# Two kilobytes of each w_gate partition moved from SyncE's DMA queue to GpSimd's, in loads of 100, 20 and 8 rows

## The chip, the cores and the metric

The kernel runs on one core of a Trainium2 chip (trn2). Such a core has TensorE (PE), which multiplies matrices, VectorE (DVE), ScalarE (ACT), GpSimd (POOL) and SyncE (SP), and 16 DMA engines that carry data between the chip's memory (HBM) and the on-chip memory of 128 partitions (SBUF). A DMA is issued by SP, ACT or POOL, and each of them has a queue of its own onto the DMA engines. The metric is device time in microseconds (us) of one execution; lower is better.

## The reference

One token of a decoder block, everything in fp32: LayerNorm, attention over a cache of 65536 positions with 8 key/value heads and 4 query heads to each, a residual, a second LayerNorm, and a gated feed-forward layer with no nonlinearity in it. `norm` stands for the LayerNorm of the reference.

```python
D, Hq, Hkv, Sk, Dh, F = 512, 32, 8, 65536, 128, 1792
q = norm(x) @ wq                       # 32 query heads of 128
scores = einsum("bhqd,bhkd->bhqk", q, repeat(k_cache, 4)) * Dh ** -0.5
o = einsum("bhqk,bhkd->bhqd", softmax(scores), repeat(v_cache, 4))
h = x + o.reshape(1, 1, Hq * Dh) @ wo
n = norm(h)
h2 = h + ((n @ w_gate) * (n @ w_up)) @ w_down
```

Keys and values are 256 MiB each; all else together is under 30 MiB.

## The kernel before

**Main part.** TensorE runs one loop of eight turns, one for each key/value head (`head()`, L330 to L388). In each turn four tiles of keys (line L343) and four of values (L371) are read, each tile 128 partitions by 64 KB, through two buffers `kv[0]` and `kv[1]`. SP issues the loads of these tiles (L131, and L127 for the last tile of values, which comes in four pieces cut by `V_CUTS`), each as soon as TensorE has read the tile before last in the same buffer. Between the key tiles and the value tiles lies a softmax shared by ACT, DVE and PE.

**The tail.** After the last head the two buffers are used again for the feed-forward weights. `wg_t` and `wu_t` (w_gate and w_up) lie in `kv[0]`, `wd_t` (w_down) in `kv[1]`. In `wg_t` a partition holds 28 KB, which is four blocks `k` of 1792 floats. SP issues w_gate as one DMA (L137) once PE has finished the third value tile of the last head (`pe_at(LAST, M_V + 2)`), and right behind it w_up in three pieces (L140); w_down follows in five pieces (L144) once PE has finished the fourth value tile. The pieces are cut by `U_CUTS` and `D_CUTS`, and each has a semaphore of its own.

TensorE's order in the tail is written out by hand: the second LayerNorm (L393, L395), `project()` with w_gate (L406, which waits for `s_wg` ahead of its first matmul), the variance (L412), a residual term (L414), `project()` with w_up (L406 again, with a wait for each piece), a transposition of the product (L418 to L425), four filling matmuls (L312), and the product with w_down (L437), which waits for each piece of w_down in turn. DVE copies the result (L297) and SP stores it (L299). SP then clears the semaphores, which ends the program.

**GpSimd.** Its work is all at the start: it fills the identity matrix and the padded tiles (L147 to L155), and it has no instruction after that. It issues no DMA. The only DMA that isn't SP's is the load of `x_row` by ACT (L109).

Of the kernel before, what the change touches and what calls it, by code (L numbers as in the profile page):

```python
# [8 lines left out]
P = 128  # L9
D = 512  # L10
# [5 lines left out]
KT = D // P  # L16
F = 1792
# [4 lines left out]
LAST = HKV - 1  # L22
PE_ONLY = bass.OrderedEngineSet([mybir.EngineType.PE])
V_CUTS = (0, 16, 24, 28, 32)
U_CUTS = (0, 2, 3, 4)
D_CUTS = (0, 6, 10, 12, 13, 14)


M_Q, M_K, M_MX, M_MB, M_T, M_L, M_V, M_PO, M_AT, M_HEAD = 1, 2, 6, 7, 8, 12, 13, 17, 18, 18
# [11 lines left out]
        return self.n  # L41


def body(nc, xr, kT, v, wq0, wqo, wo7, wg, wu, wd, out):
    pe_e, dve_e, act_e, pool_e, sp = nc.tensor, nc.vector, nc.scalar, nc.gpsimd, nc.sync

    def tile(name, *shape, align=32):
        return nc.alloc_sbuf_tensor(name, list(shape), F32, align_bytes=align).ap()
# [12 lines left out]
    f_pad = tile("f_pad", P, NC, 32)  # L61
    sel_pad = tile("sel_pad", P, 32)
    zeros = tile("zeros", P, 512)

    kv = [tile(f"kv{i}", P, CK, align=1024) for i in range(2)]
    wqo_sb = tile("wqo_sb", P, 2, KT, 512, align=1024)
# [22 lines left out]
    def sem(name):  # L89
        sems.append(nc.alloc_semaphore(name))  # L90
        return sems[-1]

    pe, dve, act, pool = (Counter(sem(n)) for n in ("pe", "dve", "act", "pool"))
    tok, atok = sem("tok"), sem("atok")
    s_kv = [sem("s_kv0"), sem("s_kv1")]
    s_wq, s_w = sem("s_wq"), sem("s_w")
    s_vp = [sem(f"s_vp{i}") for i in range(len(V_CUTS) - 1)]
    s_wg = sem("s_wg")
    s_wu = [sem(f"s_wu{i}") for i in range(len(U_CUTS) - 1)]
    s_wd = [sem(f"s_wd{i}") for i in range(len(D_CUTS) - 1)]  # L100
    s_xr, s_out = sem("s_xr"), sem("s_out")
    wg_t, wu_t = kv[0][:, 0:KT * F], kv[0][:, KT * F:2 * KT * F]
    wd_t = kv[1]

    def pe_at(h, m):
        return M_HEAD * h + m


    act_e.dma_start(x_row, xr).then_inc(s_xr, 16)  # L109

# [2 lines left out]
    for h in range(HKV):  # L113
        for i in range(2 * NT):
# [9 lines left out]
            if h == LAST and i == 2 * NT - 1:  # L124
                for p, (lo, hi) in enumerate(zip(V_CUTS, V_CUTS[1:])):
                    cs = slice(lo * 512, hi * 512)
# [7 lines left out]
                    sp.sem_inc(p, 16)  # L134
            done.append(pe_at(h, M_K + i if i < NT else M_V + i - NT))
    sp.wait_ge(pe.sem, pe_at(LAST, M_V + 2))
    sp.dma_start(wg_t, wg).then_inc(s_wg, 16)  # L137
    for p, (lo, hi) in enumerate(zip(U_CUTS, U_CUTS[1:])):
        cs = slice(lo * F, hi * F)
        sp.dma_start(wu_t[:, cs], wu[:, cs]).then_inc(s_wu[p], 16)  # L140
    sp.wait_ge(pe.sem, pe_at(LAST, M_V + 3))
    for p, (lo, hi) in enumerate(zip(D_CUTS, D_CUTS[1:])):
# [7 lines left out]
        out=ident, in_=ident, compare_op=ALU.not_equal, fill=1.0, base=0,  # L150
# [2 lines left out]
        c_zero = pool.tick(pool_e.memset(t, 0.0))  # L153
    for t in (o_pad, hn_pad, f_pad, sel_pad, acc):
        c_pads = pool.tick(pool_e.memset(t, 0.0))  # L155

    def dve_self():
        dve_e.wait_ge(dve.sem, dve.n)
# [16 lines left out]
        out=xd, in0=x_col, scalar1=ln_m[:, 0:1], scalar2=None, op0=ALU.subtract))  # L175
# [10 lines left out]
        out=xn, in0=xd, scalar1=ln_r[:, 0:1], scalar2=None, op0=ALU.mult))  # L186
# [3 lines left out]
        out=sel_h, in_=ident.rearrange("p (g h) -> p h g", h=REP), axis=AX.X, op=ALU.add))  # L190
    dve.tick(dve_e.tensor_reduce(
        out=sel_b, in_=ident.rearrange("p (j c) -> p c j", j=4)[:, 0:16, :], axis=AX.X, op=ALU.add))
# [5 lines left out]
        out=neg_mean, in0=mean_m, scalar1=sel_1[:, 0:1], scalar2=-1.0, op0=ALU.mult, op1=ALU.mult))  # L198
# [7 lines left out]
    for h in range(HKV):  # L206
# [7 lines left out]
        for s in range(NT):  # L214
# [11 lines left out]
            out=mrow, in_=sm[1][0:1, 0:P].rearrange("p (g h) -> p h g", h=REP), axis=AX.X, op=ALU.max))  # L226
# [4 lines left out]
            out=nbias, in0=sm[0][:, 0:1], scalar1=-SCALE, scalar2=None, op0=ALU.mult))  # L231
# [6 lines left out]
        for s in range(NT):  # L238
# [7 lines left out]
            out=l4, in0=sel_h, scalar1=l1[:, 0:1], scalar2=None, op0=ALU.mult).then_inc(tok, 1)  # L246
# [7 lines left out]
            out=o_pad[:, :, 0], in0=sm[0][:, 0:REP], in1=linv, op=ALU.mult).then_inc(tok, 1)  # L254
# [12 lines left out]
        out=arow, in0=attn, scalar=1.0, in1=acc, op0=ALU.mult, op1=ALU.add, accum_out=rsum[:, 0:1]))  # L267
    dve_self()
    c_nmean = dve.tick(dve_e.tensor_scalar(
        out=nmean, in0=neg_mean, scalar1=rsum[:, 0:1], scalar2=None, op0=ALU.mult))  # L270
# [16 lines left out]
    for half in range(2):  # L287
        cs = slice(half * 256, min(FJ, half * 256 + 256))
        c_f.append(dve.tick(dve_e.scalar_tensor_tensor(
            out=f_sb[:, cs], in0=psc[0][:, cs], scalar=ln_r3[:, 0:1], in1=g_sb[:, cs],  # L290
# [6 lines left out]
    c_y = dve.tick(dve_e.tensor_copy(y, pva[:, 0:P]))  # L297
    sp.wait_ge(dve.sem, c_y)
    sp.dma_start(out, y[0:P:32, :]).then_inc(s_out, 16)  # L299
    sp.wait_ge(s_out, 16)  # L300

    nums = [s.num for s in sems]
# [27 lines left out]
    def head():  # L330
# [33 lines left out]
        for n in range(NT):  # L364
            vt = kv[n % 2]
            pieces = list(zip(V_CUTS, V_CUTS[1:])) if n == NT - 1 else [(0, 32)]
            for p, (lo, hi) in enumerate(pieces):
# [30 lines left out]
    def project(acc, w, sems):  # L398
        for k in range(KT):
            if len(sems) == 1 and k == 0:  # L400
                pe_e.wait_ge(sems[0], 16)
            elif len(sems) > 1 and k in U_CUTS:
                pe_e.wait_ge(sems[U_CUTS.index(k)], 16)
            for j in range(4):
                o = k * F + j * FJ
                i = mm(acc[32 * j:32 * j + 32, :FJ], hn_pad[:, k, :], w[:, o:o + FJ],  # L406
                       start=(k == 0), stop=(k == KT - 1))
        i.then_inc(pe.sem, 1)

    project(psc[1], wg_t, [s_wg])  # L410
    pe_e.wait_ge(dve.sem, c_s3)
    mm(sm[0][:, 0:1], mean_m, ln_s3, start=True, stop=True).then_inc(pe.sem, 1)  # L412
    for j in range(4):
        mm(pva[32 * j:32 * j + 32, 0:P], sel_pad, arow[:, j * P:(j + 1) * P], start=True, stop=False)  # L414
    project(psc[0], wu_t, s_wu)
    pe_e.wait_ge(dve.sem, c_f[0])
    for b in range(2):
# [63 lines left out]
```

## Time and profile before

| what | value |
|---|---|
| time, median of 3 runs | 1309.85 us (1309.78 to 1309.93) |
| profiled execution, its own time | 1309.92 us |
| its span in the trace | 1308.5 us |
| data read from HBM | 564.66 MB, 432 GB/s over the span |
| TensorE, matmuls | busy 712.9 us, 54% of the span |
| DVE, ACT, POOL | busy 73.5, 47.2 and 2.5 us |
| mean granted clock of TensorE | 0.738 |

The page divides the span into 40 slices and gives for each the busy share of the engines and of the 16 DMA engines. "SPq" is SP in its role as a DMA queue's issuer, "ACTq" that of ACT. The chain of waits follows the last instruction back through what released each step. A row of the windows view gives, for one stretch, the busy time and number of instructions of each engine, the granted clock of TensorE, the mean busy share of the 16 DMA engines and the rate in GB/s. "q1", "q8" and so on are queues on the DMA engines; the kind "instruction" is the fetch of program code.

### The profile page before, as it was taken

How to read it: one execution, taken by the hardware profiler on the slowest of the kernel's cores; microseconds unless marked ns; L12 is line 12 of the kernel's file. 1: busy time of each engine (PE TensorE's matmuls, PEld its weight loads, DVE VectorE, ACT ScalarE, POOL GpSimd, SP SyncE). 2: the span in 40 equal slices, each digit the busy share in tenths (PEclk: the TensorE clock that was granted, in tenths of full speed). 3: DMA queues.
4: the chain of work that ended last, by engine and by line, in shares of the span. 5: the costliest groups of instructions: out<-in, count | busy, mean ns of one | idle time of the engine just before them, and what ended most of it. 6: DMA issues, size and time to landing. Idle time of an engine off the chain costs nothing. (4 is left out here: it accounts for less than half of the span.)

```text
span 1308.5 us, 10559 instructions
## 1 busy us (share of the span) xinstructions
PE 712.9 (54%) x4938; PEld 249.0 (19%) x4938; DVE 73.5 (6%) x181; ACT 47.2 (4%) x102; POOL 2.5 (0%) x13
## 2 busy tenths in 40 slices
PE   5366384553755446563564636636365465655556
PEld 3012031210312112120131202212021121311113
DVE  0000000100001000010000100001000010000101
ACT  0000000100001000010000100001000010000100
POOL 0000000000000000000000000000000000000000
PEclk9777666776767867767767867678677677687778
DMA  9999999999999999999999999999999999999998
GB/s 417 427 435 445 421 445 425 441 425 441 425 441 425 441 429 441 441 429 437 429 439 427 441 425 441 427 441 437 435 435 431 439 417 450 425 441 425 441 420 374
DMA packets 12260, 564.80 MB, mean 432 GB/s; under 512 B 1365, under 2 KB 1369, under 8 KB 2010
## 3 DMA queue, kind: packets, MB, share of 16 engines
q1 hardware_dynamic: 12248, 564.67, 99.7%
q8 instruction: 6, 0.10, 0.0%
q14 instruction: 4, 0.03, 0.0%
q10 hardware_dynamic: 2, 0.00, 0.0%
HBM read 564.66 MB, written 0.00 MB: 432 GB/s over the span
## 5 line engine op out<-in xcount | busy, mean ns | idle before, releaser
L343 PE MATMUL psc<-kv,q_pad 128*32 128x512 f32 x2048 | 294.6, 740 | 256.2 <-PEq L315 256.2
L371 PE MATMUL pva<-kv,pt 128*16 128x512 f32 x2048 | 280.1, 707 | 276.9 <-PEq L315 276.8
L343 PEld LDWEIGHTS psc<-kv,q_pad 128*32 128x32 f32 x2048 | 81.3, 133 | 463.0 <-issue 463.0
L371 PEld LDWEIGHTS pva<-kv,pt 128*16 128x16 f32 x2048 | 67.1, 110 | 492.7 <-issue 492.7
L210 ACT COPY sc<-psc 128x512 f32<-128x512 f32 x32 | 18.7, 585 | 1144.3 <-PE psc L343 1144.3
L216 DVE TENSOR_REDUCE mx<-sc 128x1 f32<-128x512 f32 x32 | 21.9, 686 | 538.3 <-ACT sc L210 538.3
L333 PEld LDWEIGHTS sm<-xn,wqo_sb 128*128 128x128 f32 x256 | 49.1, 299 | 10.4 <-issue 10.4
L333 PE MATMUL sm<-xn,wqo_sb 128*128 128x1 f32 x256 | 49.8, 329 | 2.2 <-issue 2.2
L250 DVE COPY orow<-pva 128x512 f32<-128x512 f32 x8 | 5.5, 692 | 566.8 <-PE pva L371 566.8
L358 PE MATMUL ptp<-ident,sc 128*128 128x128 f32 x128 | 29.3, 396 | 10.2 <-PEq L315 9.7
L358 PEld LDWEIGHTS ptp<-ident,sc 128*128 128x128 f32 x128 | 21.4, 202 | 15.5 <-issue 14.7
L235 ACT ACTIVATE sc<-sc,nbias 128x512 f32<-128x512 f32 x32 | 22.7, 711 | 20.2 <-DVE nbias L230 20.2
L240 DVE COPY pt<-ptp 128x512 f32<-128x512 f32 x32 | 22.1, 691 | 21.6 <-PE ptp L358 21.6
L363 PE MATMUL pva<-zeros 128*32 128x512 f32 x64 | 12.9, 890 | 0.0
L384 PE MATMUL attn<-wqo_sb,o_pad 128*32 128x512 f32 x64 | 10.8, 749 | 3.4 <-PEq L315 3.4
L378 PE MATMUL sm<-sel_b,orow 128*128 128x4 f32 x64 | 8.2, 252 | 7.2 <-PEq L315 7.2
L378 PEld LDWEIGHTS sm<-sel_b,orow 128*128 128x128 f32 x64 | 7.7, 191 | 14.4 <-issue 14.4
L349 PE MATMUL sm<-ident,m 128*1 128x128 f32 x8 | 2.2, 269 | 13.6 <-PEq L315 13.6
L406 PE MATMUL psc<-kv,hn_pad 128*32 128x448 f32 x64 | 8.2, 651 | 1.9 <-DMA kv<-in_wu 1.0
L361 PE MATMUL sm<-l,ones 128*128 128x4 f32 x16 | 3.9, 312 | 9.6 <-PEq L315 9.6
L351 PE MATMUL sm<-ones,mexp 1*128 1x1 f32 x16 | 3.4, 279 | 5.7 <-PEq L315 5.7
L235 ACT ACTIVATION_READ_ACCUMULATOR sc<-sc,nbias 128x1 f32 x32 | 6.0, 187 | 0.0
(88 smaller groups left out, 68.6 us busy)
## 6 DMA issues: line engine op xcount, KB each, us to landing
wqo_sb<-in_wqo SPq DMA_DIRECT2D x7, 2048.0 KB, 15.2
kv<-in_v SPq DMA_DIRECT2D x1, 4096.0 KB, 21.7
kv<-in_wg SPq DMA_DIRECT2D x1, 3584.0 KB, 18.8
kv<-in_v SPq DMA_DIRECT2D x1, 2048.0 KB, 26.2
kv<-in_v SPq DMA_DIRECT2D x2, 1024.0 KB, 29.1
kv<-in_wu SPq DMA_DIRECT2D x1, 1792.0 KB, 23.0
kv<-in_wu SPq DMA_DIRECT2D x2, 896.0 KB, 25.5
kv<-in_wd SPq DMA_DIRECT2D x1, 1536.0 KB, 19.7
```

Source lines behind the costliest of these rows:

```text
L210: copies.append(act.tick(act_e.copy(sc[s], psc[s % 2])))
L216: i = dve_e.tensor_reduce(out=mx[:, s:s + 1], in_=sc[s], axis=AX.X, op=ALU.max)
L235: act_e.activation(sc[s], sc[s], AF.Exp, bias=nbias[:, 0:1], scale=SCALE, accum_out=sums[:, s:s + 1]).then_inc(atok, 1)
L240: dve_e.tensor_copy(pt[s].rearrange("p g b h -> p b g h"), ptp[s % 2].rearrange("p (b g h) -> p b g h", b=4, h=REP)).then_inc(tok, 1)
L333: i = mm(sm[0][:, r:r + 1], wq_sb[:, k, r * P:(r + 1) * P], xn[:, k:k + 1], start=(k == 0), stop=(k == KT - 1))
L343: i = mm(psc[s % 2][32 * j:32 * j + 32, :], q_pad[:, 28 - 4 * rs:60 - 4 * rs], kv[s % 2][:, (4 * rs + j) * 512:(4 * rs + j + 1) * 512], st ...
L358: i = pe_e.transpose(ptp[s % 2][:, b * P:(b + 1) * P], sc[s][:, b * P:(b + 1) * P], ident)
L363: mm(pva[32 * j:32 * j + 32, :], zeros[:, 0:32], zeros, start=True, stop=False)
L371: i = mm(pva[32 * j:32 * j + 16, :], pt[n][:, 8 * j + rs, :, :].rearrange("p b h -> p (b h)"), vt[:, w * 512:(w + 1) * 512], start=False, ...
L378: i = mm(sm[0][:, 0:REP], orow[:, b * P:(b + 1) * P], sel_b[:, 4 * b:4 * b + 4], start=(b == 0), stop=(b == 3))
L384: i = mm(attn[32 * r:32 * r + 32, :], o_pad[:, r, :], wo_sb[:, r, :], start=True, stop=True)
L406: i = mm(acc[32 * j:32 * j + 32, :FJ], hn_pad[:, k, :], w[:, o:o + FJ], start=(k == 0), stop=(k == KT - 1))
```

## The change

Of each partition's 28 KB of w_gate, 26 KB are still loaded by SP, and 2 KB by GpSimd. A partition's row is seen as two halves of 14 KB (`halves`). SP's load takes the first 13 KB of both halves, still as one DMA, and GpSimd's take the last 1 KB of both. GpSimd's part is cut by partitions into three loads, of rows 0 to 99, 100 to 119 and 120 to 127. Ahead of each goes a tiny load of 13, 6 and 6 rows of 32 bytes (two runs of 16 bytes each) from a view of x into a tile `spare` that nobody reads. GpSimd waits for the same point of TensorE's count as SP does for w_gate. The wait of `project()` for w_gate becomes two: one for `s_wg`, one for the three loads of `s_wx`. At the end of the program SP also waits for the tiny loads.

```diff
+SHARED = KT * F // 2 - 256
+EXTRA = ((0, 100), (100, 120), (120, P))
...
+    spare = tile("spare", 16, len(EXTRA), 2, 2 * KT)
...
+    def halves(t):
+        return t.rearrange("p (a f) -> p a f", a=2)
...
     sp.wait_ge(pe.sem, pe_at(LAST, M_V + 2))
-    sp.dma_start(wg_t, wg).then_inc(s_wg, 16)
+    sp.dma_start(halves(wg_t)[:, :, :SHARED], halves(wg)[:, :, :SHARED]).then_inc(s_wg, 16)
...
+    pool_e.wait_ge(pe.sem, pe_at(LAST, M_V + 2))
+    for n, (lo, hi) in enumerate(EXTRA):
+        r = 6 if n else 13
+        pool_e.dma_start(spare[0:r, n, :, 0:KT], xq[0:r]).then_inc(s_sp, 16)
+        pool_e.dma_start(halves(wg_t)[lo:hi, :, SHARED:], halves(wg)[lo:hi, :, SHARED:]).then_inc(s_wx, 16)
...
     sp.dma_start(out, y[0:P:32, :]).then_inc(s_out, 16)
+    sp.wait_ge(s_sp, 16 * len(EXTRA))
     sp.wait_ge(s_out, 16)
...
             if len(sems) == 1 and k == 0:
                 pe_e.wait_ge(sems[0], 16)
+                pe_e.wait_ge(s_wx, 16 * len(EXTRA))
...
+        "xq": lay(A_x, D // 8, 2, 4),
```

More of the change, by code (lines that the diff above doesn't have):

```diff
@@ L41, in tick, with body @@
         return self.n
-def body(nc, xr, kT, v, wq0, wqo, wo7, wg, wu, wd, out):
+def body(nc, xr, xq, kT, v, wq0, wqo, wo7, wg, wu, wd, out):
     pe_e, dve_e, act_e, pool_e, sp = nc.tensor, nc.vector, nc.scalar, nc.gpsimd, nc.sync
@@ L100, in body @@
     s_wd = [sem(f"s_wd{i}") for i in range(len(D_CUTS) - 1)]
-    s_xr, s_out = sem("s_xr"), sem("s_out")
+    s_xr, s_out, s_wx, s_sp = (sem(n) for n in ("s_xr", "s_out", "s_wx", "s_sp"))
     wg_t, wu_t = kv[0][:, 0:KT * F], kv[0][:, KT * F:2 * KT * F]
```

## The prediction

> **What bounds the kernel now.** I read the page first: its slices, its DMA queues and its chain of waits.
>
> ```profile
> span 1308.5 us, 10559 instructions
> ...
> DMA  9999999999999999999999999999999999999998
> ...
> q1 hardware_dynamic: 12248, 564.67, 99.7%
> q8 instruction: 6, 0.10, 0.0%
> q14 instruction: 4, 0.03, 0.0%
> ...
> DMA kv<-in_wd 2%; SPq L144 0%; PE pva L371 0%; PE pva L437 0%; DVE y L297 0%
> ```
>
> The DMA engines are busy from the first slice to the last, nearly all of it with SP's queue (q1). So the time is that of the transfers, and what an edit can change is how many bytes there are (they stay the same) and how the 16 engines come to their end. The chain of waits in order of time shows that end.
>
> ```profile
> 1283.06 22.84 DMA kv<-in_wd
> 1305.90 0.04 issue
> 1305.94 0.47 PE pva L437 x8
> 1306.41 0.02 issue
> 1306.44 0.29 DVE y L297
> ```
>
> The last piece of w_down lands at 1305.90; four matmuls, a copy and the store follow, 2.6 us to the end of the span, and the change touches none of them. The windows view, in steps of a fifth of a microsecond, shows how the engines get there; the column before the last is their mean busy share.
>
> ```profile
> 200.00:1255.00 1055.00, 567.84 (x3883) 191.16 (x3883) 57.10 (x128) 37.60 (x84) 0.00 (x0) 0.73 1.00 434
> 1303.00:1304.00 1.00, 0.53 (x20) 0.53 (x24) 0.00 (x0) 0.00 (x0) 0.00 (x0) 1.00 1.00 393
> 1304.00:1304.20 0.20, 0.20 (x18) 0.20 (x12) 0.00 (x0) 0.00 (x0) 0.00 (x0) 1.00 0.97 338
> 1304.20:1304.40 0.20, 0.20 (x16) 0.09 (x4) 0.00 (x0) 0.00 (x0) 0.00 (x0) 1.00 0.48 184
> 1304.40:1304.60 0.20, 0.16 (x8) 0.00 (x0) 0.00 (x0) 0.00 (x0) 0.00 (x0) 1.00 0.46 174
> 1304.60:1304.80 0.20, 0.10 (x4) 0.11 (x8) 0.00 (x0) 0.00 (x0) 0.00 (x0) 1.00 0.37 143
> 1304.80:1305.00 0.20, 0.20 (x12) 0.20 (x15) 0.00 (x0) 0.00 (x0) 0.00 (x0) 1.00 0.40 154
> 1305.00:1305.20 0.20, 0.20 (x14) 0.07 (x4) 0.00 (x0) 0.00 (x0) 0.00 (x0) 1.00 0.37 143
> 1305.20:1305.40 0.20, 0.20 (x12) 0.07 (x8) 0.00 (x0) 0.00 (x0) 0.00 (x0) 1.00 0.19 72
> 1305.40:1305.60 0.20, 0.20 (x8) 0.09 (x8) 0.00 (x0) 0.00 (x0) 0.00 (x0) 1.00 0.08 31
> 1305.60:1305.80 0.20, 0.16 (x8) 0.00 (x0) 0.00 (x0) 0.00 (x0) 0.00 (x0) 1.00 0.00 0
> ```
>
> They don't end together. Until 1304.2 all sixteen work; then 0.48 of them, which is eight; from 1304.6 on 0.37, which is six; and these six stop between 1305.2 and 1305.6. So eight are early (done at about 1304.2), two in the middle (1304.55), six late (the last at 1305.57). The end of the kernel waits for the latest of the six, which is 1.4 us behind the early ones. Why six are late shows in a window of 4 us of the DMA queues.
>
> ```profile
> q1 hardware_dynamic: 112, 1.49, 88.8%
> q8 instruction: 1, 0.02, 1.4%
> q14 instruction: 1, 0.01, 0.5%
> ```
>
> From 1286 to 1290 two fetches of code come in between SP's packets. A fetch is one packet, so it holds one engine: 1.4% of 16 engines times 4 us is 0.90 us for some 16 KB (0.10 MB in 6 packets), 0.5% is 0.32 us for 8 KB. The sixteen shares of a load are equal, so an engine that has fetched code stays behind the others to the end. I read the late six as those that fetched the 16 KB packets, the middle two as those with 8 KB; the trace doesn't number its engines, so that is a reading, not a row.
>
> **The change part by part.** Only the order and place of 256 KB changes (128 partitions of 2 KB), out of 564.66 MB.
>
> *Bytes.* SP's load of w_gate gets shorter by 2 KB in each of 8 rows to an engine, 16 KB on all sixteen. At 434/16 = 27.1 GB/s for an engine that is 0.60 us less on each. GpSimd's loads give the 256 KB back, and all depends on which engines take them. The ends are these: if no late engine takes any, the late ones gain 0.60 us; if the 256 KB go evenly to all sixteen, nothing is gained; if a late engine takes more than its share, the end moves back. Here the row counts speak. 100, 20 and 8 rows can be dealt as 10 and 2 rows to ten engines and 1 row to eight of these: 13 rows at most, 26 KB, and 24 KB for the two that go without the last. If GpSimd's queue goes round the sixteen engines from load to load, with 13 engines for the tiny load of 13 rows and 6 for one of 6, then 13 + 10 = 23 leaves it at engine 7, 6 more at 13 again, and each of the three data loads begins at the same place. So the same six in a row are left out, and in the windows six are late. I take this value: late engines 0.60 us less, early and middle ones 10 and 8 KB more, 0.38 and 0.30 us.
>
> [...] No row here shows a DMA of GpSimd's.
>
> *Packets.* Small packets cost something of their own: in the window from 1303 to 1304, in which w_down comes in packets of 2 and 4 KB, the engines are fully busy at 393 GB/s in place of 434. For 2 KB that is 83 ns in place of 76, so some 8 ns for a packet. SP's w_gate has 16 pieces to an engine in place of 8, 0.06 us on every engine. GpSimd's 24 to 26 pieces of 1 KB on the ten engines are 0.2 us.
>
> *Breaks.* A second queue breaks into SP's stream. The nearest rows are the fetches, from both sides: a middle engine is 0.35 us behind an early one for a fetch that was itself 0.32 us long, so nearly nothing beyond it; a late one is 1.0 to 1.4 us behind for one of 0.90, so 0.1 to 0.5 us beyond. GpSimd's packets are small, like the former, and I take 0 to 0.1 us a break. Each engine sees about three of them: the ten have the data loads, the six in a row that are left out have the tiny loads.
>
> *Sum.* A late engine ends at 1305.57 - 0.60 + 0.06 + (0 to 0.3) = 1305.03 to 1305.33, a middle one at 1304.55 + 0.30 + 0.06 + 0.19 + (0 to 0.3) = 1305.10 to 1305.40, an early one sooner. The last of them is 0.17 to 0.47 us earlier than 1305.57. I take 0.35, and the work behind it moves along. On the profiled execution's 1309.92 (span 1308.5 and 1.4 around it) that is 1309.57; the median of the runs lies 0.07 below it, so 1309.5.
>
> *The added waits.* TensorE's `project` now also waits for GpSimd's loads, and everything behind it in TensorE's order (the variance, w_up, w_down) is queued behind that wait. The rows that bear on it are of the timeline, the waits, the DMA issues (KB each, and us to landing) and the timeline's start.
>
> ```profile
> 1269.72 0.33 SPq L137 DMA_DIRECT2D kv<-in_wg  x1
> ...
> 1288.68 4.78 PE L406 MATMUL psc<-kv,hn_pad 128*32 128x448 f32 x32 [0.87 <-DMA kv<-in_wg]
> ```
>
> ```profile
> PE pva L437 <- DMA kv<-in_wd: 1.0, 2, 0.8
> PE psc L406 <- DMA kv<-in_wu: 1.0, 1, 1.0
> ```
>
> ```profile
> kv<-in_wg SPq DMA_DIRECT2D x1, 3584.0 KB, 18.8
> ...
> kv<-in_wu SPq DMA_DIRECT2D x2, 896.0 KB, 25.5
> ...
> wqo_sb<-in_wq SPq DMA_DIRECT2D x1, 1024.0 KB, 4.8
> ```
>
> ```profile
> 0.73 0.52 ACTq L109 DMA_DIRECT2D x_row<-in_xr  x1
> ```
>
> GpSimd is released when SP is, at 1269.7, and has nothing else to do. The first matmul with w_gate starts at 1288.68, so the loads have 19 us. Behind that TensorE idles 1.0 us for w_up and 1.0 for w_down, so up to some 2 us of lateness would still be hidden: the loads must land by 1290.7. No row shows what GpSimd takes to issue a DMA. The nearest are 0.33 (SP) and 0.52 us (ACT): six issues make 2 to 3 us, and to landing an unburdened 1 MB takes 4.8. The other end is a load that stands behind all that SP has queued, like w_up's last pieces, 25.5 us. I take the near end, since the fetches above came through within SP's stream, while w_gate was still on its way; then the wait costs nothing, and w_gate itself (18.8 us to landing) stays what `project` waits for. [...] SP's new wait at the end is for loads 20 us old and costs nothing.
>
> **The rivals.**
>
> *The shares fall on late engines.* If GpSimd's loads are dealt to all sixteen in runs of 7, 2 and 1 rows, an engine takes up to 10 rows, 20 KB for the 16 it lost, 0.15 us more; if the round begins elsewhere than in the sum, a late engine takes up to 26 KB, 0.38 more. With 0.06 and 0.2 for packets and up to 0.3 for breaks the end is 0.4 to 0.9 us later: 1310.5. For it: that the trace shows no engine numbers. Against it: six and six. In this case the change doesn't do what its row counts say.
>
> *Breaks are dear.* At 0.5 us a break, the upper end above, three breaks put a middle engine at 1305.10 + 1.5 = 1306.6, 1.0 us later than now: 1310.9. From 0.16 us a break on the change loses; once the breaks on one engine sum to over 3.1 us (a little over six at 0.5), the kernel is slower by over 2.6 us. If each of the 24 pieces were a break, it would be 12 us: 1321. For it: the lateness of 1.0 to 1.4 us for fetches of 0.90. Against it: the middle engines.
>
> *The gate waits for GpSimd.* If its loads get their turn only behind w_up, they land 25.5 us after 1271 or so, and 0.6 later themselves, at 1297 to 1298, in place of 1288.7. Less the 2 us hidden that is 7 us: 1317. It decides from a landing at 1290.7 on, and passes 2.6 us at 1293.3. Against it stand the fetches that went in between SP's packets.
>
> **How the numbers follow.** A difference of 0.2%, 2.6 us, is about what a measurement of this kernel can tell from no change. The forecast, 1309.5 with its own range of 1309.3 to 1309.7, has 0.50; the shares on late engines (1310.5) 0.22; dear breaks 0.17, of which 0.09 with few of them (1310.9) and 0.08 beyond 2.6 us; the gate's wait (1317) 0.07; things not thought of 0.04. Within 0.2% lie the forecast, the first rival, the cheap half of the second and half of the rest: 0.83. Slower are 0.08 and 0.07: 0.15. Faster by 2.6 us can't come from the balance, where the early engines bound the gain at 1.4 us: 0.02. The range goes from 1309.1, the 0.60 us whole and the spread of the runs, to 1311.4, a second rival with four breaks; it leaves out the gate's wait and the many breaks, under 0.2 in all.
>
> **What would show it.** In the changed trace a queue of GpSimd's appears, with 256 KB; the share of busy engines falls later than 1304.2 by some 0.5 us, and the step of 0.37 gets shorter or is gone; the last landing of w_down comes at about 1305.5. The wait ahead of the first L406 is for SP's w_gate and not for GpSimd's part. I am wrong if the step of six late engines is as long as before (shares dealt otherwise), if the rate from 1270 to 1290 falls below 430 GB/s by more than a per cent (breaks), or if TensorE starts w_gate after 1290.7.

## The result, and the profile after

The changed kernel takes 1311.55 us (median of 22 runs, 1311.23 to 1312.39), the kernel before 1309.89 (median of 22 runs beside them): 1.66 us more, ratio 1.0013, interval 1.0007 to 1.0019. The prediction was 1309.5, with a range of 1309.1 to 1311.4; the time lies 0.15 above the range. The profiled execution took 1311.59, its span is 1310.2. The page of the kernel after, its head, DMA queues and chain:

```profile
span 1310.2 us, 10566 instructions
...
q1 hardware_dynamic: 12376, 564.40, 99.6%
q0 software_dynamic: 256, 0.26, 0.1%
q8 instruction: 6, 0.10, 0.0%
q14 instruction: 4, 0.03, 0.0%
...
DMA kv<-in_wd 2%; PE pva L385 0%; SPq L151 0%; PE pva L452 0%; DVE y L310 0%
```

GpSimd's queue is q0, with its 0.26 MB. The end is the same work as before, the last landing of w_down, only later, in the chain in order of time:

```profile
1286.11 21.39 DMA kv<-in_wd
1307.50 0.04 issue
1307.55 0.47 PE pva L452 x8
1308.02 0.02 issue
1308.04 0.29 DVE y L310
```

1307.50 stands against 1305.90. The windows view of the end (the column before the last is the share of busy DMA engines):

```profile
1304.80:1305.20 0.40, 0.40 (x24) 0.40 (x19) 0.00 (x0) 0.00 (x0) 0.00 (x0) 1.00 0.87 343
1305.20:1305.60 0.40, 0.40 (x24) 0.40 (x20) 0.00 (x0) 0.00 (x0) 0.00 (x0) 1.00 0.74 287
1305.60:1306.00 0.40, 0.40 (x25) 0.40 (x17) 0.00 (x0) 0.00 (x0) 0.00 (x0) 1.00 0.52 200
1306.00:1306.40 0.40, 0.40 (x24) 0.40 (x19) 0.00 (x0) 0.00 (x0) 0.00 (x0) 1.00 0.30 113
1306.40:1306.80 0.40, 0.40 (x24) 0.38 (x16) 0.00 (x0) 0.00 (x0) 0.00 (x0) 1.00 0.19 72
1306.80:1307.20 0.40, 0.40 (x20) 0.16 (x8) 0.00 (x0) 0.00 (x0) 0.00 (x0) 1.00 0.06 20
```

All engines end later than before, the first ones as well (1304.8 in place of 1304.2), and instead of three groups they end one by one, over 2.4 us. Added up over these windows and those of the kernel before, the sixteen engines end on average 1.2 us later than before, the last one 1.6. Where this comes from shows in two windows of 3 us and a wide one, first of the kernel before, then after (the last column is GB/s):

```profile
1276.00:1279.00 3.00, 2.23 (x20) 0.29 (x12) 0.00 (x0) 0.00 (x0) 0.00 (x0) 1.00 1.08 457
1279.00:1282.00 3.00, 1.05 (x8) 0.16 (x8) 0.69 (x1) 0.00 (x0) 0.00 (x0) 1.00 1.10 475
...
1270.00:1300.00 30.00, 21.64 (x174) 8.73 (x174) 3.47 (x12) 0.90 (x2) 0.00 (x0) 0.89 1.00 426
```

```profile
1276.00:1279.00 3.00, 1.21 (x12) 0.13 (x4) 0.00 (x0) 0.00 (x0) 0.00 (x0) 1.00 1.02 329
1279.00:1282.00 3.00, 1.86 (x8) 0.16 (x8) 0.00 (x0) 0.00 (x0) 0.00 (x0) 0.56 1.05 375
...
1270.00:1300.00 30.00, 22.83 (x156) 8.34 (x156) 2.49 (x9) 0.90 (x2) 3.77 (x6) 0.72 1.01 409
```

Over these 30 us the engines are as busy as before and deliver 17 GB/s less: 510 KB, which at 434 GB/s is 1.17 us. It is lost while GpSimd's loads are under way: 329 and 375 GB/s with every engine busy (shares of 1.02 and 1.05), in place of 457 and 475 (1.08 and 1.10). So the engines don't wait; their packets take longer.

The timeline of GpSimd and the first matmul with w_gate settle the added wait:

```profile
1270.59 0.70 POOL L167 DMA_DIRECT2D spare<-in_xq  x1 [1267.35 <-PE pva L385]
1271.28 0.80 POOL L168 DMA_DIRECT2D kv<-in_wg  x1
...
1273.79 0.57 POOL L168 DMA_DIRECT2D kv<-in_wg  x1
...
1292.80 5.00 PE L421 MATMUL psc<-kv,hn_pad 128*32 128x448 f32 x32 [0.26 <-DVE hn_pad L285]
```

```profile
kv<-in_wg POOLq DMA_DIRECT2D x1, 200.0 KB, 7.7
kv<-in_wg POOLq DMA_DIRECT2D x1, 40.0 KB, 8.0
...
kv<-in_wg POOLq DMA_DIRECT2D x1, 16.0 KB, 8.6
```

GpSimd's last load lands at 1273.79 + 8.6 = 1282.4. TensorE starts w_gate at 1292.80 and waits there for DVE, not for a load.

### The profile page after: what moved, and what is told of

Its sections match the earlier page's. It is cut to its first block, busy times and chain, and to the rows that moved or that the text cites. A ratio compares the mean times of both kernels' runs of the same rounds, so it can differ in the third digit from the quotient of the medians.

```text
span 1310.2 us, 10566 instructions
## 1 busy us (share of the span) xinstructions
PE 716.3 (55%) x4938; PEld 249.2 (19%) x4938; DVE 73.5 (6%) x181; ACT 47.2 (4%) x102; POOL 6.2 (0%) x19
## 3 DMA queue, kind: packets, MB, share of 16 engines
q1 hardware_dynamic: 12376, 564.40, 99.6%
```

## The experiments

The theories. **A**: GpSimd's queue breaks into SP's stream, and that costs per packet or per load. **B**: its bytes fell on engines that were late already. **C**: SP's split of w_gate, or (**C'**) TensorE's later start in the tail. **D**, formed after the first four runs: a load of other than all 128 rows gives an engine other partitions to write than SP's loads of 128 rows do, and writes of two engines to the same partitions hold each other up. Each experiment is an edit of the changed kernel, but for the last two. Medians stand against the kernel before, run beside them (1309.94, 1309.85 and 1309.81 us for the first four, the next four and the last three).

With eleven runs the interval of a ratio reaches about 0.0009, which is 1.2 us, to either side, so by the intervals alone a loss of 1.1 us isn't told from none. What tells them apart is that the runs hardly overlap: in the change and the four edits of it that are said to lose, every run took 1310.63 us or more; in the five that are said not to, 51 of 55 runs took less. The rate in the windows goes the same way.

**SP loads the rest.** GpSimd's six loads are left out:

```diff
+    sp.dma_start(halves(wg_t)[:, :, SHARED:], halves(wg)[:, :, SHARED:]).then_inc(s_wx, 16)
```

> GpSimd issues nothing; SP loads the 2 KB of each partition itself, as one more DMA of 128 rows behind its 26 KB. Theory A (a second queue's packets break into SP's stream and the engines deliver less while they do): no second queue, so only the small packets remain, 1309.9 to 1310.2 us, and the rate from 1276 to 1282 stays at 450 GB/s or more. Theory B (GpSimd's bytes fell on late engines): equal shares, 1309.9. Theory C (splitting w_gate in two runs of 13 KB and a remainder costs by itself): most of the change's loss stays, 1311 or more.

Measured: 1310.09, ratio 1.0001 (0.9992 to 1.0010). The rate from 1276 to 1282 was 443 and 438 GB/s, somewhat under the 450 expected, but the time is that of the kernel before: the split and the small pieces are not the loss, and C falls.

**Only the tiny loads.** SP loads w_gate whole; of GpSimd's loads the three of `spare` stay.

> Only the three tiny loads by GpSimd; SP loads w_gate whole, as before. Theory A, if every packet of the second queue costs alike: about half of the loss, 1310.5 to 1310.8 us, with a dip of the rate behind 1274. Theory A, if only packets with data cost: 1309.9 to 1310.1. Theory B: no bytes moved, 1309.9.

Measured: 1310.27, ratio 1.0001 (0.9992 to 1.0010), between the two cases of A; an effect of some tenths isn't told from none.

**No tiny loads.** The loads of 100, 20 and 8 rows stay.

> The three data loads by GpSimd without the tiny loads ahead of them. Theory A, if every packet costs alike: 1310.6 to 1311.0 us; if packets with data cost: 1311.3 to 1311.6, as with the tiny loads. Theory B: another division over the engines, so a time that differs from the change's 1311.55 by 0.3 or more, either way.

Measured: 1311.08, ratio 1.0010 (1.0001 to 1.0019). Between the two cases of A, and 0.47 from the change, as B allows: it didn't separate them. It shows that most of the loss (1.14 of 1.66 us) comes with the data.

**One load of 128 rows**, no tiny loads.

```diff
-EXTRA = ((0, 100), (100, 120), (120, P))
+EXTRA = ((0, P),)
```

> One load of all 128 rows by GpSimd, no tiny loads: every engine gets 8 rows, what it lost. Theory A: the same 256 KB in packets of the second queue, a loss of 0.8 to 1.5 us, 1310.7 to 1311.4. Theory B: equal shares, 1309.9 to 1310.1.

Measured: 1310.17, ratio 1.0001 (0.9992 to 1.0010). The same 256 KB by the same queue cost 0.23 us, which isn't told from nothing, so A in the form "packets of a second queue" falls. The window of this kernel:

```profile
1270.00:1300.00 30.00, 23.36 (x164) 8.73 (x164) 2.50 (x9) 0.89 (x2) 0.83 (x1) 0.77 1.01 426
```

426 GB/s, as before the change. B would say that equal shares cure it; D that the rows are each engine's own. The next experiments tell these apart.

**Two loads of 64 rows**, no tiny loads: by the row counts equal shares, of other rows. That is the author's estimate: the traces don't number the engines, so none shows which rows an engine takes.

```diff
+EXTRA = ((0, 64), (64, P))
```

> GpSimd's 256 KB as two loads of 64 rows, no tiny loads: again 8 rows for each of sixteen engines, but an engine now has other rows (4 of each load) than those that SP's load of 128 rows gives it. Theory D (partitions: a write costs when an engine writes partitions that another engine is writing to, as the load of 128 rows doesn't do): SP's packets behind 1274 get longer than their 309 ns, the rate falls under 400 GB/s for some 5 us, and 0.6 to 1.5 us are lost, 1310.6 to 1311.5. Theory A (packets of a second queue) and theory B (shares): as with the one load of 128 rows, 1309.9 to 1310.3.

Measured: 1310.92, ratio 1.0009 (1.0000 to 1.0018): 1.07 us of loss with shares that are equal by the row counts, as D has it and neither A nor B. Its profiled execution took 1312.56, 1.64 above the median, so its window (393 GB/s) overstates the loss:

```profile
1270.00:1300.00 30.00, 21.23 (x160) 7.81 (x156) 2.50 (x9) 0.90 (x2) 1.31 (x2) 0.83 1.01 393
```

**Three loads of 128 rows with the tiny loads**: six loads by GpSimd, as in the change, cut by columns.

```diff
+EXTRA = ((0, 0, 256), (1, 0, 128), (1, 128, 256))
...
+        cs = slice(SHARED + lo, SHARED + hi)
...
+        pool_e.dma_start(halves(wg_t)[:, a, cs], halves(wg)[:, a, cs]).then_inc(s_wx, 16)
```

> GpSimd's 256 KB as three loads of all 128 rows, cut by columns (1 KB, 512 B and 512 B of a row), with the same three tiny loads ahead of them: six loads in GpSimd's queue as in the change, but every engine writes the rows that SP's loads give it. Theory D: only the tiny loads and the more pieces cost, 1310.0 to 1310.6, packets of SP stay near 309 ns. Theory A (number of loads and breaks): the change's loss, 1311.0 or more.

Measured: 1309.97, ratio 1.0001 (0.9992 to 1.0010).

```profile
1270.00:1300.00 30.00, 22.97 (x177) 8.78 (x169) 3.31 (x11) 0.89 (x2) 3.51 (x6) 0.83 1.01 426
```

Six loads of GpSimd's, 256 KB, and no loss that can be told: neither the number of loads, nor the tiny ones, nor the queue is the cause.

**SP issues the three loads itself**, GpSimd none.

```diff
+    for lo, hi in EXTRA:
+        sp.dma_start(halves(wg_t)[lo:hi, :, SHARED:], halves(wg)[lo:hi, :, SHARED:]).then_inc(s_wx, 16)
```

> SP itself issues the three loads of 100, 20 and 8 rows behind its 26 KB of w_gate; GpSimd issues nothing. Theory D: no second queue, and yet engines write other engines' partitions, so a loss of 0.6 to 1.5 us, 1310.6 to 1311.5, with SP's packets longer around them. Theory A: no second queue, so no loss but by the shares, 1309.9 to 1310.3.

Measured: 1311.41, ratio 1.0016 (1.0007 to 1.0025), nearly the change's loss without a second queue. It comes later, where these loads stand in SP's queue. The windows of this kernel are these; before, the first two had 369 and 404 GB/s, but with the engines busy for 0.86 and 0.97 of the time only:

```profile
1285.00:1288.00 3.00, 2.30 (x10) 2.21 (x10) 0.86 (x5) 0.00 (x0) 0.00 (x0) 0.50 1.05 358
1288.00:1291.00 3.00, 0.68 (x4) 0.23 (x8) 0.25 (x2) 0.00 (x0) 0.00 (x0) 0.50 1.01 349
...
1270.00:1300.00 30.00, 21.24 (x164) 7.89 (x164) 2.50 (x9) 0.90 (x2) 0.00 (x0) 0.83 1.01 413
```

**GpSimd's six loads some 470 us earlier**, into a tile `wx` of their own, copied into place in the tail.

```diff
+    pool_e.wait_ge(pe.sem, pe_at(4, M_V + 2))
...
+        pool_e.dma_start(wx[lo:hi], halves(wg)[lo:hi, :, SHARED:]).then_inc(s_wx, 16)
+    pool_e.wait_ge(s_wx, 16 * len(EXTRA))
+    pool_e.wait_ge(pe.sem, pe_at(LAST, M_V + 2))
+    c_wx = pool.tick(pool_e.tensor_copy(halves(wg_t)[:, :, SHARED:], wx))
```

> GpSimd's six loads as in the change, but in the fifth head, some 600 us earlier, into a tile of their own, while SP's packets are of 64 KB; GpSimd copies the tile into place behind the wait that released its loads before. Theory D: the same writes to the same partitions, so the same engine time is lost, and the time is 1310.8 to 1311.6. Theory C' (in the tail the last value tile lands later, TensorE gets to w_gate 4 us later and its order becomes the bound): nothing of the tail moves, 1309.4 to 1310.2.

Measured: 1312.23, ratio 1.0018 (1.0009 to 1.0027). C' falls: with only GpSimd's copy in the tail, where C' had 1310.2 at most, the loss is there, even larger (2.4 us, above the 1.0 to 1.8 that D had). In the window in which these loads run, first this kernel, then the kernel before:

```profile
795.00:840.00 45.00, 28.15 (x176) 12.81 (x176) 2.40 (x5) 0.59 (x1) 3.08 (x5) 0.73 1.02 422
```

```profile
795.00:840.00 45.00, 25.40 (x176) 11.40 (x176) 2.39 (x5) 0.58 (x1) 0.00 (x0) 0.75 1.02 441
```

19 GB/s over 45 us are 855 KB, 2 us. The change, whose loads come later, has 441 GB/s in this window like the kernel before; but the rate differs between windows without such loads too (431 in the kernel before from 700 to 795 and from 840 to 930), so the 2 us are an upper end. Between SP's packets of 64 KB the three loads landed 22 to 37 us after their issue, in place of 8; that the rate is low for longer because of it is a reading.

**Even and odd rows**: two loads of 64 rows again, but every second partition.

```diff
+        pool_e.dma_start(halves(wg_t)[n::2, :, SHARED:], halves(wg)[n::2, :, SHARED:]).then_inc(s_wx, 16)
```

> As with two loads of 64 rows by GpSimd, but one of the even and one of the odd partitions: each engine gets 4 rows of every load, four even or four odd ones out of eight neighbours. If theory D holds and the load of 128 rows gives an engine eight neighbouring partitions (D1), these are its own rows and nothing is lost: 1309.9 to 1310.3, GpSimd's packets of 4 KB at 159 ns. [...]

Measured: 1309.90, ratio 1.0001 (0.9992 to 1.0010), and the undisturbed rate in the wide window:

```profile
1270.00:1300.00 30.00, 22.88 (x177) 8.58 (x169) 3.07 (x11) 0.90 (x2) 1.35 (x2) 0.83 1.00 426
```

So a load of 64 rows costs nothing by itself; which 64 decides. D1 fits, but the next pair speaks against it. Which rows an engine gets in such a load stays open.

**Eight more loads of 8 rows by SP**, an addition of 512 KB to the kernel before, into an unused part of the buffer: once with rows four apart, as below, once with neighbours, `rows = slice(8 * n, 8 * n + 8)`.

```diff
+    for n in range(8):
+        rows = slice(32 * (n // 4) + n % 4, 32 * (n // 4) + 32, 4)
+        sp.dma_start(kv[0][rows, 2 * KT * F:], v[0, 0][rows, 2 * KT * F:]).then_inc(s_id, 16)
```

> The kernel before, with eight more loads by SP behind w_up, of 8 rows of 8 KB each into an unused part of the buffer (512 KB more in all): the rows of a load are four partitions apart, and the loads cover partitions 0 to 63. Eight engines get 64 KB more each, 2.4 us. [...] D1: rows of others, some 2 us more on top, 1313 to 1315.

> The same eight loads and bytes, but each of eight neighbouring partitions. [...] If rows don't matter: the same time as with the rows four apart, within 0.4 us.

Measured: 1312.75 (ratio 1.0022, 1.0012 to 1.0031; ten runs, 1313.14 at most) and 1315.07 (1.0039, 1.0023 to 1.0054; four runs, 1314.63 at least). The queue, the number of loads, their rows, bytes and packets (12376 in q1) are the same; 2.3 us lie in which rows. The window in which these loads run, first four apart, then neighbours:

```profile
1295.00:1304.00 9.00, 7.00 (x76) 3.77 (x72) 1.31 (x5) 0.89 (x2) 0.00 (x0) 0.88 1.01 422
```

```profile
1295.00:1304.00 9.00, 6.73 (x59) 3.81 (x58) 1.31 (x5) 0.89 (x2) 0.00 (x0) 0.85 1.02 336
```

422 GB/s is the undisturbed rate here (421 in the kernel before); with neighbours it is 336, all engines busy (a share of 1.02). The loads of 64 rows go the same way: as blocks of neighbours, rows 0 to 63 and 64 to 127, they lost 1.07 us, as every second row nothing that could be told. Of D it leaves that the rows decide, whichever queue carries them; that an engine must keep to rows of its own was not shown.

By what the rows decide, no run shows. Nor does one separate writing from reading: in all of them the rows in HBM changed together with the partitions.

Rows four apart came out at 1312.75, 0.25 below the range of D1 (from 1313), too little for the time to decide against it; the rate, no lower than without the loads, speaks against D1. In both kernels TensorE's product with w_down (6.03 and 6.13 us, at a granted clock of 0.50) ends the chain. It begins when the first piece of w_down lands, at 1303.48 and at 1305.57, so 2.09 of the 2.3 us are those of the landing.

## Why the prediction was wrong

*What bounds the kernel*: right. The DMA engines decide, and the end moved with the last landing of w_down, by 1.60 us.

*Bytes*: this step failed. It counted only how many bytes each engine carries and took every engine to write any partition at 27.1 GB/s. The runs show that it matters which rows a load covers. In loads of all 128 rows or of every second one GpSimd's 256 KB cost nothing that can be told from noise (one load, 1310.17; three loads, 1309.97; even and odd rows, 1309.90). In blocks of neighbouring rows they cost 1.07 (two loads of 64) to 1.56 us (SP's own three loads). The term that was missing is 1.17 us in the change. The other 0.4 of the 1.60 by which the last landing moved is a wider spread of the engines' ends, whose cause is open. Since no term stood for the loss, a gain of 0.60 on the late engines, if there was one, couldn't show. Whether it can be had in this way at all, no run shows.

*The shares*: the packet counts settle half of it. The difference of the last two numbers of these lines is the number of packets from 2 to 8 KB, in the kernel before, with one load of 128 rows, and with the loads of 100, 20 and 8 rows alone:

```profile
DMA packets 12260, 564.80 MB, mean 432 GB/s; under 512 B 1365, under 2 KB 1369, under 8 KB 2010
```

```profile
DMA packets 12468, 564.80 MB, mean 432 GB/s; under 512 B 1381, under 2 KB 1385, under 8 KB 2090
```

```profile
DMA packets 12548, 564.80 MB, mean 431 GB/s; under 512 B 1457, under 2 KB 1461, under 8 KB 2170
```

These are 641, 705 and 709, so one load of 128 rows makes 64 packets, each of 4 KB, the data of two rows, and the three loads make 68. Ten engines with 10 rows (five packets each), ten with 2 rows and eight with 1 row (one packet each) make 50 + 10 + 8 = 68; runs of 7, 2 and 1 rows would make 57 + 10 + 8 = 75. So the counts fit the division that the prediction took. Whether the engines left out were the six late ones is not settled: the loss spreads over all engines, and no count names an engine. That GpSimd's loads leave out the late engines, on which the sum's 0.60 us less for these and its 0.38 and 0.30 more for the others rest, no run shows; the runs showed the 68 packets, and all sixteen engines at their end later, by 1.2 us on average.

*Packets and breaks*: nothing speaks against their sizes. Predicted were 0.26 us and up to 0.3; six loads across all rows cost 0.12 in all (ratio 1.0001, 0.9992 to 1.0010), too little to tell the terms from zero. GpSimd's pieces of 1 KB weren't packets of their own, as the prediction had them: four make one.

*The added wait*: right that it costs nothing. GpSimd's issues took 0.56 to 0.80 us, 3.8 us in all where 2 to 3 were estimated, and its loads landed by 1282.4, eight microseconds before the limit of 1290.7. The part that was overlooked lies ahead of it: the last piece of values, in the queues beside GpSimd's loads, landed later (TensorE begins on it at 1282.36 in place of 1280.16), and TensorE came to w_gate 4.1 us later, with the granted clock at 0.50 from 1282 to 1293. So the sign that the prediction named, w_gate begun after 1290.7, came, but not by a wait for GpSimd. Most of TensorE's idle time behind w_gate is used up by that: it waits 0.5 us for w_down and not at all for w_up. The early loads show that the loss doesn't need it.

*The rivals*: "breaks are dear" gave 1310.9 and came nearest in time, for a wrong reason. The rate's fall between 1270 and 1290, which the prediction named as its sign, came (427 to 402 GB/s), but six loads across all rows broke into the stream as well and left the rate from 1270 to 1300 at 426, that of the kernel before. "The shares fall on late engines" gave 1310.5; two loads of 64 neighbouring rows, by the row counts equal shares, lost 1.07 us, and two of every second row nothing, so it isn't the main cause. "The gate waits" is refuted by the timeline. A rival in which it matters which rows a load covers was missing.

## What to carry to other kernels

When a DMA stream runs at full rate, spread a side load evenly over the partitions. Cutting it by columns cost nothing that could be told here (1309.97 against 1309.85), nor did cutting it into even and odd rows (1309.90 against 1309.81); cutting it into blocks of neighbouring rows cost 1.1 to 1.7 us for 256 KB beside packets of 8 to 16 KB. To find such a loss, look for windows in which the DMA engines are as busy as ever and deliver less, like the 329 GB/s at a share of 1.02 here: a low rate at full share is neither a late issue nor a wait. Before balancing engines, ask which rows each piece of work covers, besides which engine carries it.

## What the runs showed of the hardware that was not expected

Two loads of 64 rows cost 1.07 us when their rows are neighbours and nothing that can be told from noise when they are every second partition (1310.92 against 1309.90). With eight loads of eight rows in SP's queue the engines delivered 422 GB/s when the rows were four partitions apart, and 336 when they were neighbours. The same six loads cost 1.66 us between SP's packets of 8 to 16 KB and 2.4 us between packets of 64 KB; that is one pair, and no run shows that the packets' size is the reason.
